# Wider read descriptors for the key and value loads of a DMA-bound decode kernel

## The chip, the cores and the metric

The kernel runs on one core of one Trainium2 chip. The metric is the device time of one execution in microseconds. "Before" is 394.84 us, the median of three runs (394.8 to 394.9).

## The reference, cut to what matters

One token attends over a cache of 65,536 tokens, with 32 query heads on 4 key/value heads of 128 elements. A small gated mixer with one token runs beside it.

```python
Hq, Hkv, Sk, Dh = (32, 4, 65536, 128)
q = (x @ wq)...                              # 1 x 1024 times 1024 x 4096
scores = einsum('bhqd,bhkd->bhqk', q, k) * Dh ** (-0.5)
o = einsum('bhqk,bhkd->bhqd', softmax(scores), v)
a = o... @ wo                                # 1 x 4096 times 4096 x 1024
b = ...                                      # mixer: w_in 1024 x 3584, w_out 1792 x 1024
return g * a + (1 - g) * b
```

All is bf16. Keys and values are 67 MB each, the weights another 28 MB. Every byte is used once, so 162 MB have to be loaded.

## The kernel before

Everything large goes through one ring of nine slots in SBUF. A slot is 16 KB in each of 128 partitions, 2 MB in all, and holds one unit of 8,192 tokens of keys or values: partition p has tokens 64p to 64p + 63 of the unit, which lie in a row in HBM.

```python
NS = 9
SLOT = 8192                                   # bf16 elements in a partition, 16 KB
def kv(cache, g, u):
    return cache[0, g, UK * u:UK * (u + 1), :].rearrange("(p x) d -> p (x d)", p=128)
# ... cut: the list `stream` of all loads in the order of their use
def issue(upto):
    while issued[0] < min(upto, len(stream)):
        n = issued[0]
        # ... cut: an assertion
        key, src, ln = stream[n]
        s = n % NS
        P("SP", lambda e, n=n, src=src, ln=ln: e.dma_start(slot(n)[:, 0:ln], src), w=[("slot", s)], dma="s%d" % s)
        issued[0] += 1
```

A load is issued from SyncE as soon as the slot that it goes to has been used up. TensorE transposes each key tile, multiplies it with the queries, and later multiplies the exponentials with the values; VectorE and ScalarE copy and exponentiate. None of this is touched by the change.

A DMA (a transfer that runs beside the compute engines) is built as descriptors, one for each run of bytes that lie in a row: some that read from HBM and some that write to SBUF. The traces here show one record for each read; the writes are counted from the access pattern that the kernel gives for SBUF. In the kernel before, a 2 MB load is 128 reads and 128 writes of 16 KB. Shared evenly over 16 DMA engines, that is 8 and 8 per engine and load, and 512 and 512 per engine for all 64 key and value loads (64 x 128 / 16).

## Time and profile before

| what | value | view |
|---|---|---|
| span | 393.2 us | head of the page |
| DMA engines busy with the load queue | 97.3% | queue table |
| rate in the middle | 426 GB/s | windows |
| PE busy | 71% | head of the page |
| loads | 64 of keys and values (134 MB) and 14 of weights (28 MB) | DMA issues |

First the page of the kernel before, cut: the span in 40 slices (tenths busy of PE and of the DMA engines, then GB/s), and the load queue (packets, MB, share of the 16 engines' span).

```profile
PE   0438999698989867677586686879658875644543
...
DMA  8999999999999999999999999999999999999992
GB/s 324 370 429 429 425 421 434 425 426 420 427 425 427 428 425 427 421 428 427 433 423 427 427 425 427 425 430 425 427 427 427 425 428 427 425 427 427 427 395 94
...
q1 hardware_dynamic: 11240, 162.01, 97.3%
```

The DMA row is at 9 in all slices but the first and the last, while PE, the busiest compute engine, goes up and down. Next the windows of the kernel before: stretch in us, its length, busy us of each engine with the number of its instructions, granted TensorE clock, DMA share, GB/s.

```profile
30.00:120.00 90.00, 82.66 (x1153) 65.83 (x1154) 46.49 (x100) 36.59 (x41) 0.00 (x0) 0.91 1.01 426
120.00:300.00 180.00, 136.27 (x1893) 96.08 (x1889) 85.75 (x171) 68.91 (x96) 0.00 (x0) 0.91 1.01 426
300.00:360.00 60.00, 38.98 (x456) 22.82 (x460) 19.44 (x45) 17.37 (x32) 0.00 (x0) 0.71 1.01 427
```

The DMA share is 1.01 (overlapping packet records carry it over 1), so it shows no idle time in these stretches. Last, from its page, the shares of the chain of waits, and two kinds of issue (count, size, median us from issue to landing).

```profile
DMA 69%; PE 25%; DVE 4%; ACT 1%; issue 1%; SPq 0%
```

```profile
arena<-in_A_k_cache_dram SPq DMA_DIRECT2D x32, 2048.0 KB, 40.2
...
arena<-in_A_wq_dram SPq DMA_DIRECT2D x4, 2048.0 KB, 15.0
```

A load that takes 4.9 us of DMA time at 426 GB/s lands 40 us after its issue: about eight loads wait in the queue. This is why a quarter of the chain can be PE although PE does not set the time: while PE lags, the queue still has work.

### The profile page before, as it was taken

Reading aid. Unit: us, or ns where it says so; the run is one execution under the profiler, and the core shown is the slowest. Engines: PE = TensorE matmul, PEld = TensorE weight load, DVE = VectorE, ACT = ScalarE, POOL = GpSimd, SP = SyncE. Lnnn points to the kernel's source line nnn. Section 1 sums busy time; section 2 is a strip of 40 time slices with the busy share of each in tenths; the row PEclk is TensorE's granted clock in tenths of the full one; section 3 lists DMA queues with packets and bytes.
Section 4 is the critical chain, followed back from the end, with each engine's and each line's share of the span. In section 5 each row is a group of like instructions: output and inputs, shape, how many; then the busy total and the mean of one; then the engine's idle time right before and its main releaser. Section 6 shows DMA issues by size and latency. Waiting matters only on the chain.

```text
span 393.2 us, 8650 instructions
## 1 busy us (share of the span) xinstructions
PE 280.7 (71%) x3950; PEld 198.9 (51%) x3950; DVE 159.7 (41%) x357; ACT 124.3 (32%) x171; POOL 1.5 (0%) x8
## 2 busy tenths in 40 slices
PE   0438999698989867677586686879658875644543
PEld 0437888676666555555464464556435553211121
DVE  3003444475657535356354354456424454100100
ACT  1003332254565525243143242335323334210000
POOL 1000000000000000000000000000000000000000
PEclk9999888799999989899699698889988899555555
DMA  8999999999999999999999999999999999999992
GB/s 324 370 429 429 425 421 434 425 426 420 427 425 427 428 425 427 421 428 427 433 423 427 427 425 427 425 430 425 427 427 427 425 428 427 425 427 427 427 395 94
DMA packets 11852, 162.57 MB, mean 413 GB/s; under 512 B 1828, under 2 KB 1832, under 8 KB 1832
## 3 DMA queue, kind: packets, MB, share of 16 engines
q1 hardware_dynamic: 11240, 162.01, 97.3%
q8 instruction: 31, 0.51, 0.5%
q10 hardware_dynamic: 576, 0.00, 0.1%
q14 instruction: 5, 0.04, 0.0%
HBM read 162.01 MB, written 0.00 MB: 412 GB/s over the span
## 4 chain that ended last, share of the span: by engine, by line
DMA 69%; PE 25%; DVE 4%; ACT 1%; issue 1%; SPq 0%
DMA arena<-in_A_k_cache_dram 48%; PE pb L392 14%; DMA arena<-in_A_wo_dram 11%; DMA arena<-in_A_v_cache_dram 9%; PE pb L414 4%; PE pb L505 4%; DVE arena L400 2%; PE pb L459 1%; DVE arena L419 1%; ACT arena L397 0%; PE pb L600 0%; PE pb L447 0%; SPq L323 0%; PE pb L553 0%; ACT L440 0%
## 5 line engine op out<-in xcount | busy, mean ns | idle before, releaser
L392 PE MATMUL pb<-arena 128*128 128x128 bf16 x2048 | 156.1, 237 | 44.4 <-DMA arena<-in_A_k_cache_dram 44.4
L392 PEld LDWEIGHTS pb<-arena 128*128 128x128 bf16 x2048 | 134.6, 108 | 73.4 <-DMA arena<-in_A_k_cache_dram 49.3
L400 DVE COPY arena<-pb 128x1024 bf16<-128x1024 bf16 x160 | 108.3, 689 | 133.3 <-PE pb L392 132.6
L397 ACT ACTIVATE arena<-pb 128x1024 bf16<-128x1024 bf16 x96 | 97.9, 1020 | 188.2 <-PE pb L392 188.2
L414 PE MATMUL pb<-arena 128*32 128x512 bf16 x512 | 55.2, 421 | 5.3 <-DVE arena L419 3.4
L459 PE MATMUL pb<-arena 128*32 128x512 bf16 x512 | 40.1, 441 | 19.5 <-DMA arena<-in_A_v_cache_dram 19.0
L459 PEld LDWEIGHTS pb<-arena 128*32 128x32 bf16 x512 | 14.2, 104 | 33.4 <-issue 22.0
L440 ACT ACTIVATE arena<-arena 128x512 bf16<-128x512 f32 x32 | 22.8, 713 | 16.5 <-PE pb L447 14.7
L450 DVE COPY arena<-pb 128x512 bf16<-128x512 bf16 x32 | 13.6, 424 | 30.6 <-PE pb L447 30.4
L414 PEld LDWEIGHTS pb<-arena 128*32 128x32 bf16 x512 | 13.3, 93 | 21.7 <-DVE arena L419 6.2
L419 DVE TENSOR_SCALAR_CACHE_REDUCE arena<-pb 128x512 f32<-128x512 f32 x32 | 21.8, 681 | 2.8 <-PE pb L414 2.8
L447 PE MATMUL pb<-arena 128*128 128x128 bf16 x128 | 15.2, 254 | 0.0
L447 PEld LDWEIGHTS pb<-arena 128*128 128x128 bf16 x128 | 8.8, 111 | 11.6 <-issue 11.6
L505 PEld LDWEIGHTS pb<-arena 128*128 128x128 bf16 x224 | 13.8, 164 | 0.9 <-issue 0.9
L505 PE MATMUL pb<-arena 128*128 128x1 bf16 x224 | 14.1, 199 | 0.0
L600 PE MATMUL pb<-arena 128*1 128x256 bf16 x128 | 7.5, 413 | 8.6 <-DMA arena<-in_A_wo_dram 8.4
L367 PE MATMUL pb<-arena 128*128 128x1 bf16 x256 | 7.3, 165 | 5.7 <-DMA arena<-in_A_wq_dram 5.7
L352 PE MATMUL pb<-arena 128*128 128x1 f32 x2 | 0.6, 363 | 14.1 <-DVE arena L351 14.1
L367 PEld LDWEIGHTS pb<-arena 128*128 128x128 bf16 x256 | 7.2, 105 | 5.9 <-DMA arena<-in_A_wq_dram 5.9
L600 PEld LDWEIGHTS pb<-arena 128*1 128x1 bf16 x128 | 3.7, 115 | 12.1 <-DMA arena<-in_A_wo_dram 9.9
L352 PEld LDWEIGHTS pb<-arena 128*128 128x128 f32 x2 | 0.5, 313 | 14.1 <-DVE arena L351 14.1
L606 DVE TENSOR_TENSOR arena<-pb,arena 97x256 bf16<-97x256 f32 x1 | 0.4, 425 | 16.0 <-PE pb L600 16.0
(76 smaller groups left out, 53.2 us busy)
## 6 DMA issues: line engine op xcount, KB each, us to landing
arena<-in_A_k_cache_dram SPq DMA_DIRECT2D x32, 2048.0 KB, 40.2
arena<-in_A_v_cache_dram SPq DMA_DIRECT2D x32, 2048.0 KB, 38.4
arena<-in_A_wq_dram SPq DMA_DIRECT2D x4, 2048.0 KB, 15.0
arena<-in_A_wo_dram SPq DMA_DIRECT2D x4, 2048.0 KB, 42.0
arena<-in_B_w_in_dram SPq DMA_DIRECT2D x4, 1792.0 KB, 38.2
arena<-in_B_w_out_dram SPq DMA_DIRECT2D x2, 1792.0 KB, 33.9
arena<-in_A_x_dram ACTq DMA_DIRECT2D x1, 2.0 KB, 7.4
arena<-in_gate_w_dram ACTq DMA_DIRECT2D x1, 2.0 KB, 12.4
```

What stands on the lines that cost most here:

```text
L367: ins = e.matmul(pf(OB)[:, h:h + 1], sl[:, WQ_N * k + 128 * h:WQ_N * k + 128 * (h + 1)], xT[:, 2 * i + k:2 * i + k + 1], start=(i == 0 and ...
L392: ins = e.transpose(pbf(pb)[:, 128 * t:128 * (t + 1)], sl[:, 128 * (8 * b + t):128 * (8 * b + t + 1)], idb)
L397: P("ACT", lambda e, i=i, pb=pb: e.activation(ktb(i), pbf(pb), ACTF.Copy), w=[("kt", i % NKTS), B(pb)])
L400: P("DVE", lambda e, i=i, pb=pb: e.tensor_copy(ktb(i), pbf(pb)), w=[("kt", i % NKTS), B(pb)])
L414: ins = e.matmul(pf(SCB)[32 * cg:32 * (cg + 1), :], qpad[:, 128 * g + 32 * j:128 * g + 32 * (j + 1)], src, start=(j == 0), stop=(j == 3), ...
L419: P("DVE", lambda e: e.tensor_scalar(scs(n), pf(SCB), 0.0, None, op0=ALU.add, op1=ALU.max, accum_out=maxc[:, n:n + 1]), w=[("sc", n % NSC) ...
L440: P("ACT", lambda e: e.activation(psb(n), scs(n), ACTF.Exp, bias=gcol(g, K_NB), scale=SCALE, accum_out=lp[:, n:n + 1]), r=[("sc", n % NSC) ...
L447: ins = e.transpose(pbf(PTB)[:, 128 * xi:128 * (xi + 1)], psb(n)[:, 128 * xi:128 * (xi + 1)], idb)
L450: P("DVE", lambda e: e.tensor_copy(ptsb(n), pbf(PTB)[:, 0:512]), w=[("ptsb", n % 2), B(PTB)])
L459: ins = e.matmul(pf(OB)[32 * cg:32 * (cg + 1), :], ptsb(n)[:, 128 * xi + 32 * cg:128 * xi + 32 * (cg + 1)], vw(sl, 128 * (4 * cg + xi), [[ ...
L505: ins = e.matmul(pf(MB)[:, z:z + 1], vw(sl, c0, [[FC, 128]]), xT[:, 2 * i + k:2 * i + k + 1], start=(i == 0 and k == 0 and z == 0), stop=( ...
L600: ins = e.matmul(pf(FB)[32 * q:32 * q + 1, 0:QW], ovec[:, 8 * i + c:8 * i + c + 1], sl[:, DO * c + QW * q:DO * c + QW * (q + 1)], start=(i ...
```

## The change

The intent is fewer descriptors. Rows of two neighbouring partitions are neighbours in HBM too, so one read of 32 KB can feed two writes of 16 KB. Each load then has 64 reads and 128 writes, 4 and 8 per engine. The ordinary call would make both sides alike, so the instruction is built by hand. Weight loads are not touched, as their rows are not neighbours.

```diff
@@ -312,6 +312,18 @@
     for i in range(4):
         load(("wo", i), wo_v[:, 8 * i * DO:8 * (i + 1) * DO], 8 * DO)
 
+    def copy(e, dst, src):
+
+        n = dst.ap[-1][1]
+        if src.ap[0][0] != n:
+            return e.dma_start(dst, src)
+        lo = 16384
+        assert 128 * n % (16 * lo) == 0 and lo % n == 0
+        wide = bass.AP(tensor=src.tensor, offset=src.offset, ap=[[lo, 128 * n // lo], [1, lo]])
+        return e.add_instruction(mybir.InstDMACopy(
+            mode="Copy", name=nc.get_next_instruction_name(), engine=e.engine, queue="qSPDynamicHW",
+            cce_op=ALU.bypass, ins=e.lower_ap_dma(wide), outs=e.lower_ap_dma(dst)))
+
     issued = [0]
 
     def issue(upto):
@@ -320,7 +332,7 @@
             assert n < NS or stream[n - NS][0] in used
             key, src, ln = stream[n]
             s = n % NS
-            P("SP", lambda e, n=n, src=src, ln=ln: e.dma_start(slot(n)[:, 0:ln], src), w=[("slot", s)], dma="s%d" % s)
+            P("SP", lambda e, n=n, src=src, ln=ln: copy(e, slot(n)[:, 0:ln], src), w=[("slot", s)], dma="s%d" % s)
             issued[0] += 1
 
     used = set()
```

## The prediction

> **What bounds the kernel now.** The 16 DMA engines. The 40 slices of the page show DMA at 9 from the second slice to the last but one; the table of windows gives a DMA share of 1.01 and 426 GB/s from 30 to 360 us. The queue table has 162.01 MB on the load queue, busy 97.3% of the 16 engines' span. 64 of its 78 large loads (134 MB, 83%) are the key and value loads that the change touches: at 426 GB/s that is 315 of the 393.2 us. PE is busy 71%. The chain of waits names PE between 30 and 116 us (transposes of keys), but there the loads still run at 427 GB/s, because nine slots let them run ahead (issue to landing 40.2 us). So the kernel ends when the bytes have landed, plus about 6 us at the end and about 12 us of slow start, which stay.
>
> **What a load costs.** In the trace's packet records a 16 KB packet takes 613 ns (median), one of 14 KB 536, one of 512 bytes 27 to 31, a semaphore write 9. At the fabric ceiling of 435 GB/s that the Trainium skill gives (DMA: Bandwidth & Descriptors, "Where 436 GB/s comes from"), 27.2 bytes per ns and engine, 16 KB are 602 ns and 512 bytes 19. So a packet carries, by estimate, a fixed cost of 8 to 11 ns, whatever its size. With the semaphore's share that is 614 ns per packet, the 426 GB/s measured. The kernel is at 98% of that ceiling; all overhead of the touched loads is about 2% of 315 us, 6 us.
>
> **What the change does.** Each 2 MB load keeps 128 writes of 16 KB but makes 64 reads of 32 KB instead of 128 of 16 KB: per engine 4 reads and 8 writes. Bytes, slots, order of loads, semaphores and every compute instruction are the same. If the fixed 8 ns belong to the read descriptor, half of them go: 4 of 614 ns, 0.7%, 2.1 us. If they belong to the write, or the descriptors are cut at the smaller side anyway, nothing goes. I expect some 1.5 us. All of it lies on the critical path, as the DMA engines are never idle; the rate in the middle should rise from 426 to 428 to 429 GB/s. PE has room for it: after 116 us the chain already waits for loads.
>
> **The risk.** 64 reads and 128 writes must be dealt to 16 engines in the same order. The same page (section "The descriptor swizzle") gives each engine the partitions of one SBUF port for a 128-partition load. Should the changed shapes be dealt as eight consecutive partitions per engine, two engines would share a port, and the rate could fall far below 426 GB/s. No run here shows which happens. I take it at one in ten.
>
> **Prediction.** 393.3 us, range 390.0 to 396.0. Faster by over 2%: 0.03; within 2%: 0.87; slower by over 2%: 0.10.
>
> **What would show it.** Right: the load queue shows fewer or larger packets, the middle windows run at 428 to 429 GB/s, compute groups keep their mean times, the key loads land a little earlier, and the tail after the last load is unchanged. Wrong on the size: the GB/s stay at 426 (the fixed cost is not the read's), or rise to 433 and more (it hid more than the packet records show). Wrong on the risk: GB/s fall well below 400 in the middle, engines of one load land apart, and PE waits for loads longer.

## The result, and the profile after

The changed kernel takes 394.92 us, the median of four runs (394.83 to 395.01); before, in the same rounds, 394.87 us (394.80 to 394.97). The ratio is 1.0001, with a 95% interval of 0.9984 to 1.0019. A ratio here is the mean time of one kernel's fast runs over that of the other's of the same rounds, so not quite the ratio of the medians quoted. The result is correct.

The same views of the kernel after. From its page, the rate by slice and the load queue; then its windows; then the chain and the key loads.

```profile
GB/s 324 377 433 422 427 424 451 412 428 432 428 426 423 423 425 425 429 418 433 428 422 428 425 423 432 432 422 428 432 427 423 425 428 430 425 424 420 415 395 94
...
q1 hardware_dynamic: 7144, 162.01, 97.1%
```

```profile
30.00:120.00 90.00, 83.50 (x1176) 66.08 (x1177) 47.41 (x101) 37.34 (x42) 0.00 (x0) 0.91 1.01 427
120.00:300.00 180.00, 140.89 (x1870) 99.70 (x1867) 85.46 (x169) 68.17 (x96) 0.00 (x0) 0.87 1.00 427
300.00:360.00 60.00, 39.15 (x456) 22.98 (x460) 19.45 (x45) 17.36 (x32) 0.00 (x0) 0.71 1.00 427
```

```profile
DMA 69%; PE 25%; DVE 4%; ACT 1%; SPq 0%; issue 0%
```

```profile
arena<-in_A_k_cache_dram SPq DMA_DIRECT2D x32, 2048.0 KB, 40.6
```

The queue table shows 7144 packets instead of 11240, 4096 fewer: 64 loads with 64 fewer reads each. So the wide reads are real. But the windows show 427, 427 and 427 GB/s where there were 426, 426 and 427. Summed more finely from the trace's packet records between 40 and 350 us, with the bytes of each record spread evenly over its time, it is 426.24 GB/s before and 426.24 after. The shares of the chain are the same, the key loads land no earlier (40.6 us from issue), and the work on the last weights starts at 388.71 us (before: 388.78).

The packet records show where the hoped-for gain is missing. They have one record for each read descriptor:

| kernel | record | median ns | ns per 16 KB |
|---|---|---|---|
| before | 16 KB read, 16 KB write | 613 | 613 |
| after | 32 KB read, two 16 KB writes | 1227 | 613.5 |

A read of twice the size takes twice the time. The fixed part that the prediction had found in a packet did not halve with the reads.

### The profile page after: what moved, and what is told of

Same layout as the page of the kernel before. It is cut to its first block, busy times and chain, and to the rows that moved or that the text cites. A ratio compares the mean times of both kernels' runs of the same rounds, so it can differ in the third digit from the quotient of the medians.

```text
span 393.2 us, 8650 instructions
## 1 busy us (share of the span) xinstructions
PE 286.2 (73%) x3950; PEld 202.9 (52%) x3950; DVE 160.3 (41%) x357; ACT 124.3 (32%) x171; POOL 1.5 (0%) x8
## 3 DMA queue, kind: packets, MB, share of 16 engines
q1 hardware_dynamic: 7144, 162.01, 97.1%
## 4 chain that ended last, share of the span: by engine, by line
DMA 69%; PE 25%; DVE 4%; ACT 1%; SPq 0%; issue 0%
DMA arena<-in_A_k_cache_dram 48%; PE pb L404 14%; DMA arena<-in_A_wo_dram 11%; DMA arena<-in_A_v_cache_dram 10%; PE pb L426 5%; PE pb L517 4%; DVE arena L412 2%; PE pb L471 1%; DVE arena L431 1%; ACT arena L409 0%; SPq L319 0%; PE pb L612 0%; PE pb L459 0%; PE pb L565 0%; ACT L452 0%
## 5 line engine op out<-in xcount | busy, mean ns | idle before, releaser
L404 PE MATMUL pb<-arena 128*128 128x128 bf16 x2048 | 159.9, 241 | 42.5 <-DMA arena<-in_A_k_cache_dram 42.5
L404 PEld LDWEIGHTS pb<-arena 128*128 128x128 bf16 x2048 | 138.0, 109 | 72.5 <-DMA arena<-in_A_k_cache_dram 47.9
L426 PE MATMUL pb<-arena 128*32 128x512 bf16 x512 | 57.1, 436 | 4.2 <-DVE arena L431 2.3
L471 PE MATMUL pb<-arena 128*32 128x512 bf16 x512 | 40.1, 441 | 17.6 <-DMA arena<-in_A_v_cache_dram 15.9
L459 PE MATMUL pb<-arena 128*128 128x128 bf16 x128 | 15.9, 263 | 0.0
L459 PEld LDWEIGHTS pb<-arena 128*128 128x128 bf16 x128 | 9.2, 115 | 12.5 <-issue 12.4
L517 PEld LDWEIGHTS pb<-arena 128*128 128x128 bf16 x224 | 13.8, 164 | 0.9 <-issue 0.9
L379 PEld LDWEIGHTS pb<-arena 128*128 128x128 bf16 x256 | 7.2, 105 | 6.2 <-DMA arena<-in_A_wq_dram 6.2
## 6 DMA issues: line engine op xcount, KB each, us to landing
arena<-in_A_k_cache_dram SPq DMA_DIRECT2D x32, 2048.0 KB, 40.6
```

The costliest lines, as they stand in the source:

```text
L379: ins = e.matmul(pf(OB)[:, h:h + 1], sl[:, WQ_N * k + 128 * h:WQ_N * k + 128 * (h + 1)], xT[:, 2 * i + k:2 * i + k + 1], start=(i == 0 and ...
L404: ins = e.transpose(pbf(pb)[:, 128 * t:128 * (t + 1)], sl[:, 128 * (8 * b + t):128 * (8 * b + t + 1)], idb)
L426: ins = e.matmul(pf(SCB)[32 * cg:32 * (cg + 1), :], qpad[:, 128 * g + 32 * j:128 * g + 32 * (j + 1)], src, start=(j == 0), stop=(j == 3), ...
L459: ins = e.transpose(pbf(PTB)[:, 128 * xi:128 * (xi + 1)], psb(n)[:, 128 * xi:128 * (xi + 1)], idb)
L471: ins = e.matmul(pf(OB)[32 * cg:32 * (cg + 1), :], ptsb(n)[:, 128 * xi + 32 * cg:128 * xi + 32 * (cg + 1)], vw(sl, 128 * (4 * cg + xi), [[ ...
L517: ins = e.matmul(pf(MB)[:, z:z + 1], vw(sl, c0, [[FC, 128]]), xT[:, 2 * i + k:2 * i + k + 1], start=(i == 0 and k == 0 and z == 0), stop=( ...
```

## The experiments

Three theories were set against each other. Theory A: each write descriptor costs about 8 ns (9.0 in the expectations of the later runs, worked out from the earlier ones), and the reads run hidden beside the writes. Theory B: the read descriptor costs it, and what the wide reads saved was lost again elsewhere. Theory C: descriptors of this size cost nothing, and the engines move bytes at a fixed rate of 426 GB/s. In the labels r is the size of a read and w that of a write, in KB. Small reads with large writes are not among the runs: r16_w8 with its two sizes exchanged does not compile. So in every shape here the pieces of data, cut at the smaller side, are as many as the writes, and "each write costs" always also reads "each piece costs".

### Loads alone, twelve shapes

The kernel `loads` has no compute, and its output is wrong. Each stage loads 16 MB in one shape and waits for all of it, after a warm-up of 8 MB.

```diff
+ phase(e, V, 0, 16, 16, 16, 8)     # rows of 16 KB, reads of 16, writes of 16, 8 loads
+ phase(e, K, 1, 16, 32, 16, 8)
+ phase(e, V, 1, 16, 8, 8, 8)
+ phase(e, K, 2, 16, 16, 8, 8)
+ phase(e, V, 2, 16, 32, 8, 8)
+ ...                               # 4/4, 16/4, 32/4, 32/32 (4 MB loads), 16/16, 2/2, 16/2
```

> Loads alone, no compute, wrong output on purpose: 12 stages of 16 MB (after a warm-up of 8 MB), each ended by a wait for all its loads, with read/write descriptors in KB of 16/16, 32/16, 8/8, 16/8, 32/8, 4/4, 16/4, 32/4, 32/32, 16/16 again, 2/2, 16/2. 64 packets of 16 KB per engine and stage: 16/16 about 64 x 0.614 = 39.3 us plus a latency of 2 to 3 us that all stages share. Theory A, every write descriptor costs about 8 ns and the reads are hidden: 32/16 equals 16/16; 8/8, 16/8 and 32/8 are each 0.5 us longer than 16/16; the three with 4 KB writes 1.6 us longer; the two with 2 KB writes 3.7 us longer; 32/32 is 0.26 us shorter. Theory B, the read descriptor costs it: 32/16 is 0.26 us shorter than 16/16, 16/8 and 16/4 equal 16/16, 4/4 is 1.6 us longer. Theory C, no descriptor of these sizes costs anything and the engines are at a rate per byte: all stages equal within 0.1 us.

The timeline of `loads` has one line for the issues of each stage: its start in us, the time that the issuing took, and the number of loads. A stage lasts until the start of the next. The first line is the warm-up, the last the output.

```profile
0.73 2.49 SPq L20 DMA_DIRECT2D arena<-in_A_k_cache_dram  x4
23.38 5.03 SPq L20 DMA_DIRECT2D arena<-in_A_v_cache_dram  x8
65.68 4.99 SPq L20 DMA_DIRECT2D arena<-in_A_k_cache_dram  x8
107.98 15.05 SPq L20 DMA_DIRECT2D arena<-in_A_v_cache_dram  x8
151.01 5.21 SPq L20 DMA_DIRECT2D arena<-in_A_k_cache_dram  x8
193.90 5.15 SPq L20 DMA_DIRECT2D arena<-in_A_v_cache_dram  x8
236.94 25.53 SPq L20 DMA_DIRECT2D arena<-in_A_k_cache_dram  x8
281.61 20.27 SPq L20 DMA_DIRECT2D arena<-in_A_v_cache_dram  x8
325.99 20.01 SPq L20 DMA_DIRECT2D arena<-in_A_k_cache_dram  x8
370.12 2.42 SPq L20 DMA_DIRECT2D arena<-in_A_v_cache_dram  x4
411.74 5.03 SPq L20 DMA_DIRECT2D arena<-in_A_k_cache_dram  x8
454.03 31.80 SPq L20 DMA_DIRECT2D arena<-in_A_v_cache_dram  x8
500.57 30.53 SPq L20 DMA_DIRECT2D arena<-in_A_k_cache_dram  x8
547.21 0.33 SPq L67 DMA_DIRECT2D out_dram<-arena  x1
```

| read/write, KB | stage, us | against 16/16 | write descriptors more, per engine |
|---|---|---|---|
| 16/16 | 42.30 and 42.29 | | |
| 32/16 | 42.30 | 0.00 | 0 |
| 8/8, 16/8, 32/8 | 43.03, 42.89, 43.04 | +0.59 to +0.74 | 64 |
| 4/4, 16/4, 32/4 | 44.67, 44.38, 44.13 | +1.83 to +2.37 | 192 |
| 2/2, 16/2 | 46.54, 46.64 | +4.24, +4.34 | 448 |
| 32/32 | 41.62 | -0.68 | -32 |

The write size orders the stages, the read size hardly does: 32/16 equals 16/16 to 0.01 us, and 16/2 takes as long as 2/2 with an eighth of the reads. At 2 KB a write descriptor costs 4.34 us / 448 = 9.7 ns. From the other stages it is 9.2 to 11.6 ns at 8 KB and 9.5 to 12.3 at 4 KB, at all sizes more than the 8 that were expected. The packet records of this run agree: a 16 KB read takes 611 ns (median) with one write, 625 with two, 644 with four and 681 with eight. Theories B and C are out for loads alone. The three with 4 KB writes are 0.54 us apart, in the order of their read counts, as are their records (1296, 1288 and 1284 ns for 32 KB, smallest reads first). If that is the reads, it is 0.54 us / 224 = 2.4 ns for each, and the stages with 8 and with 2 KB writes do not repeat it; it stays unexplained. The stage of 32/32 also has half as many loads, and its gain is larger than the 0.26 us that theory A asked for. Its records take 1213 ns where those of 32/16 take 1222, which is 0.29 us for 32 records per engine; where the rest comes from is not shown. (The comparison is within one execution.)

### The same in the kernel: writes of 8 KB with three sizes of reads

The edit, abridged, against the kernel before, with 16, 32 and 8 KB reads:

```diff
-            P("SP", lambda e, ...: e.dma_start(slot(n)[:, 0:ln], src), ...)
+            P("SP", lambda e, ...: copy(e, slot(n)[:, 0:ln], src), ...)
+    # copy: 128 rows of n = 8192 elements, each cut into writes of WR elements
+    dap = [[row, 128], [WR, n // WR], [1, WR]]            # WR = 4096: 8 KB
+    sap = [[n, 128], [n, 1], [1, n]]                      # reads of 16 KB; r32: [[RD, 64], [RD, 1], [1, RD]]; r8: [[n, 128], [RD, 2], [1, RD]]
```

> The kernel before with key and value loads of 16 KB reads and 8 KB writes: 512 write descriptors more per engine. Theory A (writes cost 8 ns each): 4.2 us longer, about 399.1 us. Theories B (reads cost it) and C (a rate per byte): 394.9 us, as before.

> The changed kernel (32 KB reads) with its writes halved to 8 KB. Theory A: 4.2 us longer than before, about 399.1 us, the same as with 16 KB reads and 8 KB writes. Theory B (reads cost it): no longer than the changed kernel, 394.9 us. Theory C: 394.9 us.

> Key and value loads with reads and writes both of 8 KB. Theory A (writes alone): the same as the other two with 8 KB writes, about 399.1 us. Theory B (reads): 399.1 us while the other two stay at 394.9. Theory C: 394.9 us. If reads and writes both cost: longer than the two with 8 KB writes and larger reads.

| kernel | median us | ratio to before (95%) |
|---|---|---|
| r16_w8 | 399.49 | 1.0117 (1.0102 to 1.0132) |
| r32_w8 | 399.51 | 1.0118 (1.0103 to 1.0133) |
| r8_w8 | 399.65 | 1.0120 (1.0103 to 1.0137) |
| before, same rounds | 394.88 | |

The load queues of the three, in the same order, and one window of the first:

```profile
q1 hardware_dynamic: 11240, 162.01, 97.5%
```

```profile
q1 hardware_dynamic: 7144, 162.01, 97.2%
```

```profile
q1 hardware_dynamic: 19432, 162.01, 97.9%
```

```profile
120.00:300.00 180.00, 143.92 (x1841) 102.09 (x1839) 85.09 (x168) 66.18 (x93) 0.00 (x0) 0.80 1.01 420
```

Reads go from 64 to 256 for each load, the packet count from 7144 to 19432, and the three times lie within 0.16 us with intervals that overlap. The write count alone has doubled against before, and it costs 4.61 us for 512 descriptors more per engine: 9.0 ns for each. The rate falls from 426 to 420 GB/s. Theory A had asked for 399.1 us in all three, and B and C for 394.9 in at least one. Note the packet counts: r16_w8 has 11240, exactly as before, with twice the writes. The queue table counts reads, so the side that costs the time is not seen in it.

### Is it linear, and does it go the other way?

The kernel r32_w4 is the changed kernel with writes of 4 KB (`WR = 2048`).

> The changed kernel (32 KB reads) with writes of 4 KB: 1536 write descriptors more per engine than before. Theory A at 9.0 ns: 13.9 us longer than before, about 408.7 us, three times the cost of 8 KB writes. If the cost were only a step between sizes and not one per descriptor, less.

It takes 408.96 us against 395.00 in the same rounds, ratio 1.0353 (1.0339 to 1.0367): 13.96 us for 1536 descriptors, 9.1 ns for each. A window of it:

```profile
120.00:300.00 180.00, 138.07 (x1776) 99.05 (x1776) 81.48 (x161) 64.95 (x91) 0.00 (x0) 0.85 1.00 408
```

For larger writes a partition must get 32 KB in a row. The kernels d_w32 and d_w16 load two neighbouring units of keys (or values) as one, into two neighbouring slots; partition p then has tokens 128p to 128p + 127 of both units. Keys and values have the same new order, and softmax does not care about it. The ring got ten slots, and the score buffers went from twelve to nine to make room. The edit, abridged, against the kernel before:

```diff
-    NS = 9
+    NS = 10
-    NSC = 12
+    NSC = 9
-        return cache[0, g, UK * u:UK * (u + 1), :].rearrange("(p x) d -> p (x d)", p=128)
+        return cache[0, g, UK * u:UK * (u + 2), :].rearrange("(p x) d -> p (x d)", p=128)
-            load(("k", k), kv(A_k_cache, *KV[k]), SLOT)
+            if k % 2 == 0: load([("k", k), ("k", k + 1)], kv(A_k_cache, *KV[k]), 2 * SLOT)
+    rd = [[n, 128], [n, 1], [1, n]]                       # one read of 32 KB for each partition
+    wr = [[row, 128], [WR, n // WR], [1, WR]]             # d_w32: WR = 16384; d_w16: WR = 8192
+    # cut: a load is issued when every key that held its one or two slots has been used up
```

> Key and value loads of 4 MB: two neighbouring units are taken as one, so that each partition gets 32 KB in a row, read and written with one 32 KB descriptor (ring of ten slots instead of nine, nine score buffers instead of twelve to make room). The order of tokens inside a unit is another one, the same for keys and values. Theory A (9.0 ns for each write descriptor, from the runs with 8 KB writes): 256 write descriptors fewer per engine, 2.3 us, and 32 completion writes of 9 ns fewer, 0.3 us: about 392.3 us, and about 429 GB/s in the middle. Theory C or a gain that cannot be had because the rate is fixed: 394.9 us. A loss if the coarser ring makes the queue run dry.

> The same loads of 4 MB, the same ring and the same token order with 32 KB reads, but written in two descriptors of 16 KB: tells the size of the write from the size of the load. Theory A: the 2.3 us are lost again, about 394.6 us, 0.3 us of fewer completions left. If the coarser load alone brings the gain: the same as with 32 KB writes.

| kernel | median us | ratio to before (95%) |
|---|---|---|
| d_w32 | 392.57 | 0.9937 (0.9924 to 0.9951) |
| d_w16 | 394.85 | 0.9996 (0.9984 to 1.0009) |
| before, same rounds | 395.00 | |

One window each, d_w32 first:

```profile
120.00:300.00 180.00, 136.98 (x1878) 97.68 (x1877) 85.52 (x173) 67.93 (x96) 0.00 (x0) 0.88 1.00 429
```

```profile
120.00:300.00 180.00, 134.45 (x1840) 95.82 (x1840) 84.40 (x168) 66.35 (x93) 0.00 (x0) 0.85 1.01 427
```

Both are correct, and both have the same loads, ring, reads and token order; they differ in the write size alone. The difference is 2.28 us for 256 write descriptors per engine, 8.9 ns for each, and the rate goes from 427 to 429 GB/s (426.28 to 429.26 by the finer sum used above). The coarser load by itself gains nothing that the interval can tell from zero. So d_w32 is faster than the kernel before by 2.4 us or 0.6%, with an interval clear of 1. The changed kernel ran in other rounds, but within 0.05 us of the kernel before. This is the gain that the change was meant to bring, from the other side of the descriptor pair.

The packet records of 32 KB reads, put side by side over the runs, show the cost by the number of writes:

| writes for each 32 KB read | kernel | median ns of the record |
|---|---|---|
| 1 of 32 KB | d_w32 | 1216 |
| 2 of 16 KB | after | 1227 |
| 4 of 8 KB | r32_w8 | 1246 |
| 8 of 4 KB | r32_w4 | 1284 |

From two writes to eight it grows by 57 ns, 9.5 ns for each write more; from one to two by 11. (The means, 1220, 1228, 1246 and 1283 ns, give 8 for the first step and 9.2 for each write after it.) Going back from one write to none, by estimate, leaves 1206 to 1207 ns for the bytes. The Trainium skill (DMA: Bandwidth & Descriptors, "Where 436 GB/s comes from") puts the ceiling at 435 GB/s, which is 1205 ns for 32 KB on one of 16 engines, by estimate from that figure. The trace agrees, by estimate: the bytes at the ceiling, plus 10 to 11 ns of the median for each write.

## Why the prediction was right or wrong

**The time was right, one term of its sum was not.** 394.92 us lies within 390.0 to 396.0 and "within 2%" was given 0.87. The point of 393.3 us was 1.6 us too low. The range held both the full gain of 2.1 us and no gain at all, so the time alone says nothing for the mechanism: a gain was forecast and none came.

- *What bounds the kernel: right.* Full DMA engines set the time. When the experiments added or took some 9 ns a write, nearly all of it showed up in the total (the packet records give 9.5 ns a write, or 9.2 by their means, which is 4.9 or 4.7 us for 512, and r16_w8 got 4.6 us longer; the 9.0 ns worked out from that foretold r32_w4 and d_w32 to 0.3 us).
- *The fixed cost of 8 to 11 ns in a packet: right in size.* The kernels give 8.9 to 9.1 ns, the stages of `loads` with 8 to 2 KB writes 9.2 to 12.3.
- *"If the fixed 8 ns belong to the read descriptor, half of them go": this is the step that failed.* The fixed cost did not go with the reads: it follows the number of writes, 4.61 us for 512 more of them, while 64 or 256 reads for each load made 0.16 us. The prediction named this case ("If they belong to the write, or the descriptors are cut at the smaller side anyway, nothing goes") but still expected 1.5 of the 2.1 us; the measured change is 0.05 us the other way, within the noise. Which of the two halves of that sentence holds, these shapes do not tell. The trace before could not tell reads from writes, because they came in pairs of the same size; only shapes that break the pairing can.
- *"The load queue shows fewer or larger packets": right,* 7144 of 11240. It was listed as a sign of success and was none: it shows the reads alone.
- *"The middle windows run at 428 to 429 GB/s", "the key loads land a little earlier": wrong,* 427 GB/s and 40.6 us (40.2 before). The compute groups are nearly unchanged (the key transposes take 241 ns instead of 237, at a granted clock of 0.83 instead of 0.85) and so is the tail, as predicted.
- *The loss feared from two engines on one SBUF port did not come.* The rate did not fall and the result is correct. How the partitions are dealt to the engines in the changed shape, the trace does not show; only that it costs nothing.

## What to carry to other kernels

When a load stream is near its ceiling, count the descriptors of reads and writes apart: here each write to SBUF cost some 9 ns, and reads no smaller than the writes were hidden beside them or nearly so, down to 2 KB. So only longer runs in one partition helped, by laying more of the data in a row for each partition. A packet count in a profile may show one side only. A fixed cost that is read off matched pairs belongs to neither side until a run breaks the pair, and one kernel of loads alone with a stage for each shape does that in one run.

## What the Trainium skill lacked or had wrong

- DMA: Bandwidth & Descriptors, "Why small descriptors are slow (HBM only)", names a fixed overhead of about 3 cycles for each packet and 32 bytes of metadata, 16 for each side, but not which side's count sets the time. Here the time follows the writes to SBUF, 8.9 to 9.1 ns for each in the kernels, with 4 to 32 KB; fewer reads gain nothing (394.92 against 394.87 us with half of them).
- The same page ends with the advice that the tile shape decides the descriptors and says that which shape is faster has not been measured. Its two shapes, one partition or 128, were not tried here. For shapes that write all 128 partitions: writes of 32 KB 392.57 us, 16 KB 394.85, 8 KB 399.49, 4 KB 408.96, where the last two differ from the first two in the size of their loads also.
- The same page does not show how a copy is built whose reads are larger than its writes. Five kernels here have it, with correct results, issued from SyncE.
- Neither lacking nor wrong: its ceiling of 435 GB/s agrees, 429 GB/s with 32 KB writes, and the bytes alone, by estimate, take 1206 to 1207 ns for 32 KB where it gives 1205.
- Nor here: HBM Reference, "Specifications (TRN2)", has about 358 GB/s for each core when both of a pair stream and about 425 for a core that streams alone. The 426 GB/s here, from a program on one core, agrees with the second. It takes the limit of the second to be the DMA engines; that the rate here moves with the size of the writes, from 408 to 429 GB/s, fits that.
